# Attention and MLP on one core: normalised rows transposed by DMA instead of TensorE, stores and v loads moved from SyncE to ScalarE

## The chip, the cores and the metric

The kernel runs on one core of a Trainium2 chip. The metric is device time in microseconds (us). The engines of the core are TensorE (PE, matrix products), VectorE (DVE), ScalarE (ACT), GpSimd (POOL) and SyncE (SP, which only issues DMA transfers). ScalarE and GpSimd can issue transfers too. All work from queues of their own, each in program order, and meet through semaphores.

## What is computed

For 8 batches of 8 heads with 576 positions and 64 columns: causal attention with a bias from a running sum, then layer normalisation of the 512 joined columns, then a two-layer MLP with 2048 hidden columns, added back.

```python
cum    = np.cumsum(np.maximum(s, 0.0), axis=-1)
scores = where(causal, -1e9, q @ k.T / 8 + np.minimum(-(cum_i - cum_j), 0.0))
attn   = softmax(scores)
x      = (attn @ v), heads joined            # (8, 576, 512)
xn     = (x - mean(x)) / np.sqrt(var(x) + 1e-6) * g_ln
out    = x + np.maximum(xn @ w_ch1, 0.0) @ w_ch2
```

## The kernel before

The order is written out by hand: every engine runs its instructions in the order in which the program names them. The main loop has 64 slots, one for each batch and head; below, slot h of a batch means the head h = 0 to 7 of the batch whose scores are made in it.

**A slot** first runs `pre(n)`, which names loads, casts and DMA transposes due for later heads. Then come the scores of its head (L312) with their exponentials on ScalarE (L323) and the masking on GpSimd (L331), and, between them, four units of the MLP of the batch before. In the middle stands `pv_next()`: attention times v (L389) for the head two slots back, and its division on VectorE (L397 to L406).

**Layer normalisation.** When the last head of batch b is through `pv_next()`, in slot h = 1 of the next batch, VectorE makes the normalised tiles xn (L451), four of 128 rows and, for odd b, a fifth with the last 64 rows of batches b-1 and b (the mixed tile). The division by the root of the variance is left to the end: it is a factor `rstd`, a power of -0.5 that GpSimd takes (L439) right after the last xn, and that enters when the output tile yo is made (L524). Only batch 1 makes its fourth and fifth tiles a slot later.

**Transposes.** The MLP needs xn with its columns on partitions. `ln_tr` does this for each tile with four 128x128 transposes on TensorE into one PSUM tile `trx` (L484), and a copy from there to xT on VectorE (L100), or on ScalarE (L98) for batches 0 (three of four), 1 and 7. For batches 1 to 6 the tiles 0 and 1 are transposed at the end of slot 2, and 2, 3 and 4 in slot 3; for batch 7 they stand between the last MLP units of batch 6. Batch 0 has its own path (L790 to L793).

**MLP units.** A batch has 32 units in `queue`: 16 of `mlp1` (L497: four products of 512 columns into `ph`, then the ReLU on ScalarE at L507, or on VectorE at L505 for the first unit of a slot), and 16 of `mlp2` (L515: a quarter of the sum for 128 rows into `py`; each fourth unit is followed by yo on VectorE and the store of yo at L542). `ph` and `py` share two PSUM buffers. The units of mlp1 fall in slots 4 to 7, those of mlp2 in slots 0 to 3 of the next batch.

**Loads.** q and k of the later heads are loaded in rows (L164), cast by GpSimd (L176), and transposed by DMA on SyncE into `kq` (L186), four heads at a time over about five slots. The rows of v are loaded by SyncE (L139) in slots 1 to 5 and cast by GpSimd (L102) a slot later. Row loads and v loads share the six buffers of `stage`. So SyncE's queue carries row loads, v loads, DMA transposes and stores, in program order, and an instruction that waits holds up all behind it.

The order inside the slot that the change touches:

```python
lt = {2: (0, 1), 3: (2, 3, 4)}.get(h, ()) if b > 1 else ()
for t in lt:
    ln_tr(b - 1, t, "act" if b == 2 else "dve")
    if t != 1 and t != 4:
        run_units(1)
        nu -= 1
run_units(nu)
```

Of the kernel before, what the change touches and what calls it, by code (L numbers as in the profile page):

```python
# [9 lines left out]
F32 = mybir.dt.float32  # L10
# [5 lines left out]
P = 128  # L16
# [3 lines left out]
def kernel(  # L20
# [11 lines left out]
    nc = tc.nc  # L32
    B, H, S, D = q.shape
# [5 lines left out]
    NF = S // P  # L39
# [13 lines left out]
    QP = S // QT  # L53

    const = ctx.enter_context(tc.tile_pool(name="const", bufs=1))
    stage = ctx.enter_context(tc.tile_pool(name="stage", bufs=6))
    pairs = ctx.enter_context(tc.tile_pool(name="pairs", bufs=4))
    small = ctx.enter_context(tc.tile_pool(name="small", bufs=4))
    xpool = ctx.enter_context(tc.tile_pool(name="xpool", bufs=3))
# [36 lines left out]
    def copy_on(eng, out, in_):  # L96
        if eng == "act":
            nc.scalar.copy(out=out, in_=in_)  # L98
        elif eng == "dve":
            nc.vector.tensor_copy(out=out, in_=in_)  # L100
        else:
            nc.gpsimd.tensor_copy(out=out, in_=in_)  # L102
# [31 lines left out]
    def ld_v(b, t):  # L134
        if b >= B:
            return
        pn = P if t < NF else TL
        tmp = stage.tile([P, H, D], F32, name="vtmp", tag="st")
        nc.sync.dma_start(  # L139
            out=tmp[:pn], in_=v[b, :, t * P : t * P + pn, :].rearrange("h s d -> s h d")  # L140
        )
        loaded["v", b, t] = tmp
# [39 lines left out]
    def tr_rows(gam, t):  # L182
        pn = P if t < NF else TL
        r = ready.pop(("rows", gam, t))
        o = t * 2 * G * P
        nc.sync.dma_start_transpose(  # L186
            out=kq[gam % 2]
            .rearrange("p u h s -> p (u h s)")[:, o : o + 2 * G * pn]
            .rearrange("p (h s) -> p h s", s=pn),
            in_=r[0:pn].rearrange("p u h c -> p (u h c)"),  # L190
        )
# [243 lines left out]
    def ln_rstd(b):  # L435
        n = len(x_tiles(b))
        rs = rstd[:, b, 0:n]
        nc.vector.tensor_scalar_add(out=rs, in0=mvs[b][:, 0:n, 1], scalar1=1e-6)  # L438
        nc.gpsimd.tensor_tensor(out=rs, in0=rs, in1=mhalf[:, 0:n], op=ALU.pow)  # L439

    def ln_aggr(b, t):
# [31 lines left out]
    def ln_first_rstd():  # L473
        for t in range(NF):
            ln_aggr(0, t)
        ln_rstd(0)

    def ln_tr(b, t, eng="dve"):
        if (b, t) not in xns:
            return  # L480
        xn = xns.pop((b, t))
        tr = ps_t.tile([P, KD, P], BF16, name="trx", tag="tr")
        for kd in range(KD):
            nc.tensor.transpose(tr[:, kd, :], xn[:, kd * P : (kd + 1) * P], ident)  # L484
        if t < NF:
            dst = xTs[b][:, :, t * P : (t + 1) * P]
        else:
            dst = xTm[:, :, (b // 2) * P : (b // 2 + 1) * P]
        copy_on(eng, dst, tr)

    first_unit = [False]

# [46 lines left out]
    def batch_units(b):  # L539
        def of_t(t):  # L540
            def put(yo, c0, c1):
                nc.sync.dma_start(out=out[b, t * P : (t + 1) * P, c0:c1], in_=yo)  # L542
            return xb[b][:, t, :], rstd[:, b, t : t + 1], put
        return chunk_units(lambda: xTs[b], of_t)

# [7 lines left out]

    queue = []
    pend = []

    def run_units(n, dve_first=False):
        for i in range(n):
            if queue:
                first_unit[0] = dve_first and i == 0  # L560
                queue.pop(0)()

# [110 lines left out]
    def pre(n):  # L675
# [29 lines left out]
            aug(n // 4 + 1, nc.sync)  # L705
        for gam in range(NPE, NG):
            m = n - 4 * gam
            if m == -6:
                ld_rows(gam, 0), ld_rows(gam, 1)
            elif m == -5:  # L710
                cast_rows(gam, 0), cast_rows(gam, 1)
                ld_rows(gam, 2), ld_rows(gam, 3)
            elif m == -4:
                tr_rows(gam, 0), tr_rows(gam, 1)
                cast_rows(gam, 2), cast_rows(gam, 3)
                ld_rows(gam, 4)
            elif m == -3:
                tr_rows(gam, 2), tr_rows(gam, 3)
                cast_rows(gam, 4)
            elif m == -2:  # L720
                tr_rows(gam, 4)
        for nb in range(2, B):
            m = n - H * nb + (5 if nb == 2 else 7)
            if 0 <= m < NT:
                ld_v(nb, m)
            if 1 <= m <= NT:
                cast_v(nb, m - 1, "pool")

# [16 lines left out]
    for n in range(BH):  # L745
# [64 lines left out]
        if n in PAIRS:  # L810
            qk_pair(PAIRS[n], ("dve", "dve"), ("act", "act"))
        scores(b, h)
        run_units(1, True)
        if h % 2 == 0:
            scores_d(b, h // 2)
# [3 lines left out]
        if n == 9:  # L819
            bias_rows(trc)  # L820
        pend.append((b, h))
        lt = {2: (0, 1), 3: (2, 3, 4)}.get(h, ()) if b > 1 else ()
        for t in lt:
            ln_tr(b - 1, t, "act" if b == 2 else "dve")
            if t != 1 and t != 4:
                run_units(1)
                nu -= 1
        if n == 2 * H + 2:
            for t in range(3, NT):
                ln_xn(1, t)  # L830
        run_units(nu)
        if b > 1 and h == 3:
            run_units(len(queue))
            queue += batch_units(b - 1)
    pv_next()
# [3 lines left out]
    for t in range(NT):  # L839
        ln_xn(B - 1, t + 1)  # L840
        run_units(1)
        ln_tr(B - 1, t, "act")
    run_units(len(queue))
    queue += batch_units(B - 1)
    queue += mixed_units()
# [30 lines left out]
```

The softmax here doesn't subtract the row's maximum and nothing guards it: scores larger than these inputs give would overflow.

## Time and profile before

| what | value |
|---|---|
| time, median of 3 (lowest to highest) | 367.94 us (367.81 to 368.48) |
| span in the profile | 366.8 us |
| VectorE busy | 202.9 us (55%) |
| ScalarE busy | 191.3 us (52%) |
| GpSimd busy | 164.9 us (45%) |
| DMA, mean over the span | 142 GB/s, 52.17 MB |
| DMA, 190 to 220 us | 178 to 208 GB/s |
| TensorE transposes of xn | 144, in 36 tiles of four |
| copies of them to xT and xTm | 23 on VectorE, 13 on ScalarE |
| transfers of SyncE that move: stores of yo / v / rows of q and k / transposes | 37 / 30 / 110 / 55 |

How to read it: a busy share is the time in which the engine had an instruction in hand, over the whole span. The one engine near 100% is TensorE, so what counts is which of its instructions could be missed, and what it would wait for then. In the attention part (up to about 290 us) all engines work; after that come the MLP of batch 7 and that of the mixed rows, in which TensorE has nearly all the work.

### The profile page before, as it was taken

To read this page: it belongs to the slowest core of one execution; us is meant where nothing else is said; L and a number is where in the kernel's file an instruction comes from. 1 tells how busy PE (TensorE), PEld (TensorE's weight loads), DVE (VectorE), ACT (ScalarE), POOL (GpSimd) and SP (SyncE) were. 2 spreads that over 40 slices of the span, in tenths; PEclk is the share of its full clock that TensorE was granted. 3 is DMA by queue.
4 is the path that set the end of the run, shared out by engine and by line. 5 is a ranking of instruction groups with operands and counts; after the bars stand their busy time and mean duration, and the time that the engine had idled before them with its cause. 6 is when DMAs were issued, how large, how long until landed. Compare 5 with 4: busy or idle time off the path is not lost.

```text
span 366.8 us, 8315 instructions
## 1 busy us (share of the span) xinstructions
PE 355.0 (97%) x3017; PEld 197.1 (54%) x3067; DVE 202.9 (55%) x535; ACT 191.3 (52%) x367; POOL 164.9 (45%) x447
## 2 busy tenths in 40 slices
PE   8998999999999999999999999999999999999995
PEld 3677555565555555555455555555555554444444
DVE  7697789684357554944384547743675483112211
ACT  5895988467732673367534753476337522501410
POOL 8854468667633656344675563554852101000000
PEclk9999999999999999999999999999999999999999
DMA  8999999999965999599979986798830011011013
GB/s 144 162 195 178 202 211 193 163 240 176 183 146 141 206 199 181 104 215 163 188 176 213 194 183 140 189 191 182 174 102 2 0 59 57 1 58 59 0 31 86
DMA packets 156653, 52.17 MB, mean 142 GB/s; under 512 B 143641, under 2 KB 151940, under 8 KB 156612
## 3 DMA queue, kind: packets, MB, share of 16 engines
q1 hardware_dynamic: 138868, 43.08, 55.5%
q0 software_dynamic: 17344, 8.03, 18.9%
q8 instruction: 24, 0.39, 0.5%
q10 hardware_dynamic: 400, 0.52, 0.4%
q14 instruction: 17, 0.14, 0.2%
HBM read 37.11 MB, written 9.44 MB: 127 GB/s over the span
## 4 chain that ended last, share of the span: by engine, by line
PE 72%; DVE 7%; DMA 6%; SPq 4%; POOL 4%; issue 3%; ACT 3%; POOLq 0%; ACTq 0%
PE py L515 26%; PE ph L497 25%; PE pot L389 6%; SPq L164 3%; PE sc L312 3%; PE sa L312 3%; PE sb L312 3%; DMA rowtmp<-in_q_dram 2%; PE idle L568 2%; DMA vtmp<-in_v_dram 2%; DVE xn L451 2%; PE trx L484 2%; DVE stats L423 1%; POOL er L331 1%; ACT er L323 1%
## 5 line engine op out<-in xcount | busy, mean ns | idle before, releaser
L515 PE MATMUL py<-w_bf,hT 128*128 128x512 bf16 (+1 forms) x565 | 132.1, 373 | 1.6 <-DVE yo L524 0.4
L497 PE MATMUL ph<-xT,w_bf 128*128 128x512 bf16 x478 | 116.4, 379 | 1.1 <-DVE yo L524 0.2
L507 ACT ACTIVATE hT<-ph 128x512 bf16<-128x512 f32 x102 | 61.0, 598 | 64.4 <-PE ph L497 64.4
L515 PEld LDWEIGHTS <-hT 128*128 128x128 bf16 x592 | 53.5, 98 | 49.1 <-issue 0.9
L497 PEld LDWEIGHTS <-w_bf 128*128 128x128 bf16 x560 | 50.1, 97 | 51.3 <-issue 2.9
L323 ACT ACTIVATE er<-sa 128x512 bf16<-128x512 f32 x64 | 38.2, 597 | 70.9 <-PE sa L312 50.1
L331 POOL TENSOR_SCALAR_AFFINE_SELECT er<-er 128x128 bf16<-128x128 bf16 x216 | 59.7, 300 | 22.5 <-ACT er L323 22.3
L505 DVE TENSOR_SCALAR hT<-ph 128x512 bf16<-128x512 f32 x38 | 26.3, 692 | 56.7 <-PE ph L497 49.0
L176 POOL CAST rows<-rowtmp 128x512 bf16<-128x512 f32 (+1 forms) x55 | 33.5, 609 | 50.7 <-DMA rowtmp<-in_q_dram 46.0
L312 PEld LDWEIGHTS <-kq 68*128 68x128 bf16 x452 | 33.4, 97 | 27.4 <-issue 1.7
L389 PEld LDWEIGHTS <-er 128*128 128x128 bf16 x960 | 37.5, 98 | 14.9 <-issue 0.7
L389 PE MATMUL pot<-v_bf,er 128*128 128x65 bf16 x960 | 40.2, 193 | 0.5 <-PE sd L355 0.3
L397 DVE RECIPROCAL rinv<-pot 128x5 f32<-128x5 f32 x64 | 12.3, 192 | 49.2 <-PE pot L389 48.9
L323 ACT ACTIVATE er<-sc 128x512 bf16<-128x512 f32 x64 | 39.2, 612 | 0.0
L323 ACT ACTIVATE er<-sb 128x512 bf16<-128x512 f32 x64 | 38.4, 599 | 0.3 <-PE sb L312 0.2
L524 DVE SCALAR_TENSOR_TENSOR yo<-py,rstd,xb 128x512 f32<-128x512 f32 x32 | 23.9, 748 | 26.2 <-PE py L515 19.7
L399 DVE TENSOR_TENSOR xb<-pot,rinv 128x256 f32<-128x256 f32 x64 | 27.2, 425 | 2.2
L102 POOL CAST v_bf<-vtmp 128x512 bf16<-128x512 f32 (+1 forms) x30 | 18.5, 617 | 19.6 <-DMA vtmp<-in_v_dram 19.5
L439 POOL TENSOR_TENSOR rstd<-rstd,mhalf 128x4 f32<-128x4 f32 (+1 forms) x8 | 8.8, 1095 | 38.0 <-DVE rstd L438 37.9
L312 PE MATMUL sc<-kq 68*128 68x256 bf16 (+1 forms) x216 | 25.3, 229 | 0.3
L423 DVE BATCH_NORM_STATS2 stats<-xb 128x6 f32<-128x128 f32 (+2 forms) x100 | 25.3, 313 | 0.4
L312 PE MATMUL sb<-kq 68*128 68x64 bf16 (+1 forms) x172 | 24.5, 244 | 0.9 <-DMA kq<-rows 0.6
(101 smaller groups left out, 322.1 us busy)
## 6 DMA issues: line engine op xcount, KB each, us to landing
out_dram<-yo SPq DMA_DIRECT2D x32, 256.0 KB
vtmp<-in_v_dram SPq DMA_DIRECT2D x24, 256.0 KB
rowtmp<-in_k_dram SPq DMA_DIRECT2D x44, 128.0 KB
rowtmp<-in_q_dram SPq DMA_DIRECT2D x44, 128.0 KB
w_bf<-in_moe_w_ch_dram POOLq DMA_DIRECT2D x8, 512.0 KB, 10.7
kp<-in_k_dram POOLq DMA_DIRECT2D x9, 144.0 KB, 6.8
qp<-in_q_dram POOLq DMA_DIRECT2D x9, 144.0 KB, 7.0
v_bf<-in_v_dram POOLq DMA_DIRECT2D x8, 128.0 KB, 8.1
```

What stands on the lines that cost most here:

```text
L176: nc.gpsimd.tensor_copy(out=r[0:pn, :, :, 0:D], in_=loaded.pop(("rows", gam, t))[0:pn])
L312: nc.tensor.matmul(a[:, c + a0 - q0 : c + a1 - q0], lhsT=k_cols(b, h, kb), rhs=cols, start=True, stop=not (pe_mask and diag),)
L323: nc.scalar.activation(out=e[:, o : o + 512], in_=a, func=ACT.Exp, scale=scale)
L331: nc.gpsimd.affine_select(out=e[:, o : o + P], in_=e[:, o : o + P], compare_op=ALU.is_ge, fill=0.0, base=0, pattern=[[1, P]], channel_mult ...
L389: nc.tensor.matmul(pot[:, t, :], lhsT=e[:, o : o + P], rhs=vv[:, kb, h, :], start=(kb == 0), stop=(kb == last),)
L399: nc.vector.tensor_tensor(out=xb[b][:, :, hs], in0=pot[:, 0:NF, 0:D], in1=rinv[:, 0:NF].unsqueeze(2).to_broadcast([P, NF, D]), op=ALU.mult,)
L423: nc.vector.bn_stats(out=st[b][:, t, part, :], in_=x[:, lo:hi])
L497: nc.tensor.matmul(ph, lhsT=w1_bf[:, kd, fb * P : (fb + 1) * P], rhs=xT[:, kd, :], start=(kd == 0), stop=(kd == KD - 1),)
L505: nc.vector.tensor_scalar_max(out=hT[:, fb, :], in0=ph, scalar1=0.0)
L507: nc.scalar.activation(out=hT[:, fb, :], in_=ph, func=ACT.Relu)
L515: nc.tensor.matmul(py[0], lhsT=hT[:, fb, t * P : (t + 1) * P], rhs=w2_bf[:, fb, c0:c1], start=(fb == 0), stop=(fb == FB - 1),)
L524: nc.vector.scalar_tensor_tensor(out=yo, in0=py[0], scalar=rs, in1=x[:, c0:c1], op0=ALU.mult, op1=ALU.add)
```

## The change

The transposes of xn for batches 1 to 7 go from TensorE to DMA transposes on SyncE (`ln_dma`): no product, no PSUM tile, no copy. They are named at the head of slots 2 and 5 (batch 1: slots 2 and 3), for batch 7 where the TensorE transposes stood. To make room on SyncE, the stores of yo for whole batches are issued by ScalarE, each one unit after the unit that made it, and the loads of v are issued by ScalarE after the slot's exponentials, into three buffers of their own, while `stage` keeps four. GpSimd's power moves from right after the last xn (slot 1 or 2) to slot 3 (`ln_pow`), so that GpSimd's queue doesn't wait there for VectorE.

```diff
-    stage = ctx.enter_context(tc.tile_pool(name="stage", bufs=6))
+    stage = ctx.enter_context(tc.tile_pool(name="stage", bufs=4))
...
-        tmp = stage.tile([P, H, D], F32, name="vtmp", tag="st")
-        nc.sync.dma_start(
+        tmp = stage.tile([P, H, D], F32, name="vtmp", tag="v", bufs=3)
+        nc.scalar.dma_start(
...
+    def ln_pow(b):
+        n = len(x_tiles(b))
+        rs = rstd[:, b, 0:n]
         nc.gpsimd.tensor_tensor(out=rs, in0=rs, in1=mhalf[:, 0:n], op=ALU.pow)
...
+    def ln_dma(b, t):
+        if (b, t) not in xns:
+            return
+        if t < NF:
+            dst = xTs[b][:, :, t * P : (t + 1) * P]
+        else:
+            dst = xTm[:, :, (b // 2) * P : (b // 2 + 1) * P]
+        nc.sync.dma_start_transpose(out=dst, in_=xns.pop((b, t)))
...
             def put(yo, c0, c1):
-                nc.sync.dma_start(out=out[b, t * P : (t + 1) * P, c0:c1], in_=yo)
+                stores.append((out[b, t * P : (t + 1) * P, c0:c1], yo))
...
                 first_unit[0] = dve_first and i == 0
+                held = list(stores)
+                stores.clear()
                 queue.pop(0)()
+                for dst, src in held:
+                    nc.scalar.dma_start(out=dst, in_=src)
...
+            if m == -2:
+                tr_rows(gam, 4)
+        if n > 16 and n % H == 2:
+            for t in range(NF if n > 18 else 3):
+                ln_dma(n // H - 1, t)
+        if n == 19:
+            ln_dma(1, 3), ln_dma(1, 4)
+        if n > 19 and n % H == 5:
+            ln_dma(n // H - 1, 4)
...
-            if 0 <= m < NT:
-                ld_v(nb, m)
...
         scores(b, h)
+        for nb in range(2, B):
+            m = n - H * nb + (5 if nb == 2 else 7)
+            if 0 <= m < NT:
+                ld_v(nb, m)
         run_units(1, True)
...
-        lt = {2: (0, 1), 3: (2, 3, 4)}.get(h, ()) if b > 1 else ()
-        for t in lt:
-            ln_tr(b - 1, t, "act" if b == 2 else "dve")
-            if t != 1 and t != 4:
-                run_units(1)
-                nu -= 1
...
         if b > 1 and h == 3:
+            ln_pow(b - 1)
             run_units(len(queue))
...
         run_units(1)
-        ln_tr(B - 1, t, "act")
+        ln_dma(B - 1, t)
+    ln_pow(B - 1)
```

More of the change, by code (lines that the diff above doesn't have):

```diff
@@ L476, in ln_first_rstd @@
         ln_rstd(0)
+        ln_pow(0)
     def ln_tr(b, t, eng="dve"):
@@ L555 @@
     pend = []
+    stores = []
     def run_units(n, dve_first=False):
@@ L707, in pre @@
             m = n - 4 * gam
+            if m == -2:
[7 more added lines that the diff above has]
+            ln_dma(n // H - 1, 4)
+        for gam in range(NPE, NG):
+            m = n - 4 * gam
             if m == -6:
@@ L719, in pre @@
                 cast_rows(gam, 4)
-            elif m == -2:
-                tr_rows(gam, 4)
         for nb in range(2, B):
             m = n - H * nb + (5 if nb == 2 else 7)
-            if 0 <= m < NT:
-                ld_v(nb, m)
             if 1 <= m <= NT:
```

## The prediction

> **What bounds the kernel now.** I read the busy shares first, then TensorE's waits, then the timelines of one batch boundary.
>
> ```profile
> PE 355.0 (97%) x3017; PEld 197.1 (54%) x3067; DVE 202.9 (55%) x535; ACT 191.3 (52%) x367; POOL 164.9 (45%) x447
> ...
> PE   8998999999999999999999999999999999999995
> ```
>
> The first line is the busy time by engine, the second TensorE's share in 40 slices: 9 from the fourth slice to the last but one. A high share of modelled matmuls proves little alone, so I looked at what they wait for. In the list of waits TensorE's own never exceed 1.3 us in total for one cause. Those that bear on the change:
>
> ```profile
> POOL rstd L439 <- DVE rstd L438: 37.9, 7, 13.7
> PEld L312 <- DMA kq<-rows: 1.4, 2, 1.1
> PE sb L312 <- DMA kq<-rows: 0.6, 1, 0.6
> PE py L515 <- DVE yo L524: 0.4, 2, 0.2
> ```
>
> Columns: total us, times, longest. TensorE is the bound and hardly waits; time is to be had only by taking work off it. What the change takes off is seen in the timeline of TensorE for slots 2 and 3 after batch 5:
>
> ```profile
> 226.13 0.62 PE L389 MATMUL pot<-v_bf,er 128*128 128x65 bf16 x15
> 226.58 0.39 PE L484 MATMUL trx<-ident,xn 128*128 128x128 bf16 x4
> 226.81 1.03 PE L515 MATMUL py<-w_bf,hT 128*128 128x512 bf16 x4
> 227.67 0.39 PE L484 MATMUL trx<-ident,xn 128*128 128x128 bf16 x4
> ...
> 229.20 0.39 PE L312 MATMUL sc<-kq 68*128 68x256 bf16 x4
> 229.79 1.89 PE L515 MATMUL py<-w_bf,hT 128*128 128x512 bf16 x8 [0.21 <-DVE yo L524]
> ```
>
> First column start, second duration. From the start of trx to the next product are 226.81 - 226.58 = 0.23 us; other tiles give 0.22. The last line is a wait that the change will make longer.
>
> [...]
>
> **The change part by part.**
>
> *TensorE transposes removed.* Batches 1 to 7 have 4 tiles each and the odd ones a fifth: 28 + 4 = 32 tiles, times 0.222 us = **7.1 us**. All of it lies on the path, as TensorE is. The 22 VectorE copies (416 ns, 9 us) and 10 ScalarE copies (585 ns, 6 us) that go lie beside it: no gain on the path.
>
> *DMA transposes added, batches 2 to 6.* The nearest row is the transposes of kq and the loads that move with them:
>
> ```profile
> L186 SPq DMA_TRANSPOSE kq<-rows x55: 1215/1260/2791, 61.2 to 267.5; - x55
> L139 SPq DMA_DIRECT2D vtmp<-in_v_dram x30: 440/590/1761, 29.4 to 248.4; - x30
> L542 SPq DMA_DIRECT2D out_dram<-yo x32: 332/364/1099, 66.6 to 335.6; - x32
> ```
>
> These are issue times in ns, min, median, max. A kq transpose has 1024 columns, one of xn 512: between 0.63 (by columns) and 1.26 us (fixed per instruction); I take 0.65. Landing follows some 2 us after the issue ends (173.67 + 1.22 to 176.89). After batch 5 the fourth xn is ready at 227.95 (VectorE's timeline), so xT has landed by about 230.6, at the dear end 232.2. MLP1 starts at 235.04, less five transposes at 233.9. Hidden. SyncE per batch: it sheds 5 x 0.59 + 4 x 0.36 = 4.4 us and gains 4.6 x 0.65 to 1.26 = 3.0 to 5.8 us. Nor are its transposes queued behind anything worse than before:
>
> ```profile
> 224.11 0.58 SPq L139 DMA_DIRECT2D vtmp<-in_v_dram  x1
> 229.77 0.36 SPq L542 DMA_DIRECT2D out_dram<-yo  x1
> 230.22 1.33 SPq L186 DMA_TRANSPOSE kq<-rows  x1
> 231.60 0.57 SPq L164 DMA_DIRECT2D rowtmp<-in_k_dram  x1
> ```
>
> Today SyncE stands from 224.7 to 229.8 at a store that waits for yo. With the stores gone it waits for xn until 228, and the row loads behind start near 228.8 instead of 231.6. The shift lets loads run earlier. After batch 3 that same late start (store at 152.01) ended in TensorE waiting for kq between 173 and 177, about 1.5 us by the gaps in its timeline. I count **1.0 us** of it as gained; 0 to 1.5 for the range. Data is 0.13 MB a tile, 0.6 MB a batch onto about 7 MB in 38 us (183 GB/s, while windows reached 209): about 200 GB/s is wanted. Tight, not over.
>
> *Batch 1.* Its fourth xn is made in slot 2 and ends at 78.73; MLP1 starts at 81.24, less five transposes at 80.1. Issue to 79.4, landing at 81.4: TensorE waits **1.2 us** (0.8 to 2.5[...]).
>
> *Batch 7.* Fourth xn 301.45, landed by 304.1; MLP1 at 306.44 less 1.1 = 305.3. Hidden, by 1.2 us at most.
>
> *The yo wait after odd batches.* VectorE runs it behind the xn tiles:
>
> ```profile
> 228.12 0.75 DVE L451 SCALAR_TENSOR_TENSOR xn<-xm,mv,gb 128x512 bf16<-128x512 f32 x1
> 228.79 0.16 DVE L438 TENSOR_SCALAR rstd<-mv 128x5 f32<-128x5 f32 x1
> 228.99 0.75 DVE L524 SCALAR_TENSOR_TENSOR yo<-py,rstd,xb 128x512 f32<-128x512 f32 x1
> ```
>
> The py of slot 3 needs the buffer that this yo frees at 229.74. That chain hangs on the product pot of slot 1, not on the transposes, so TensorE arrives 0.44 us sooner (two transposes) and waits that much more: batches 3 and 5, **0.9 us** given back. With four tiles (even b) yo ends 0.7 us ahead of its need.
>
> *ScalarE's new issues: 30 of v, 32 of yo.* Each costs between nothing (hidden under queued work) and 0.59 or 0.36 us, SyncE's medians[...]. Where ScalarE has slack it doesn't matter. It has little at 40 to 60 us, busy 9.35 and 9.15 of 10 us, and there lie the v loads of slots 11 to 15. Bare, five of 0.59 less its idle 0.54 before the copies that TensorE waits on are 2.4 us. Later the tight place is slot 4: exponentials, a v issue, a store, an exponential, and the ReLU that frees ph, with some 0.5 us to spare against 0.95: bare 0.4 x 6 = 2.4 us. Sum 0 to 4.8; I lean to the hidden end and take **0.8 us**. The store after slot 1 of an odd batch waits for yo until 229.7 and holds the exponentials of slot 3 by a microsecond; their scores' buffers are next wanted in slot 4 (234), their attention in slot 5. Hidden.
>
> *Power two slots late, buffers.* Costs nothing: rstd is wanted by the next slot 0. It frees GpSimd from 37.9 us of waiting (13.7 of it at the end), which moves casts ahead, beside TensorE. Four row buffers suffice: loads 0 and 1 are cast a slot before load 4 wants room; a v buffer is freed two slots before its next load. One unit of delay for a store meets three yo buffers, filled a slot apart. Hidden.
>
> *Sum:* 367.9 - 7.1 - 1.0 + 1.2 + 0.9 + 0.8 = **362.7 us**.
>
> **The rivals.**
>
> *All hidden.* ScalarE's issues cost nothing, the kq wait goes entirely (1.5), and batch 1 waits no more than 0.8: 367.9 - 7.1 - 1.5 + 0.9 + 0.8 = 361.0; without the batch-1 wait 360.2. I call it 360.4.[...] Against it: batch 1's arithmetic.
>
> *ScalarE becomes a second bound.* Issues bare: 367.9 - 7.1 + 0.9 + 1.2 + 4.8 = 367.7 with no gain at kq; with 1.0 there and half of the issues bare, 364.3. I put this case at 366.0. For it: 9.8 us of work in 10 at 40 to 60 us already.
>
> *Slower: issues on ScalarE as slow as SyncE's bad ones.* If each v load holds ScalarE 1.2 us (midway from 0.59 to 1.76): early 5 x 1.2 - 0.54 = 5.5; slots 4 and 5 of five batches 10 x 0.7 = 7.0; with 2.5 for batch 1 and 0.9: 367.9 - 7.1 + 15.9 = 376.7. A starved DMA (200 of 209 GB/s) would look alike. Against it: ScalarE's own ring would hold only v and stores, and 15 of the 30 loads fall in slots 1 to 3, where it is busy 3 to 4 of 10 us.
>
> **How the numbers follow.** The forecast 0.57, all hidden 0.20, second bound 0.13, slower 0.10. The range leaves out the slower case, a tail of the second bound and the edge of all hidden: 359.8 to 367.0. Slower by over 0.2% (368.7): 0.10. Within: 0.04, from the second bound. Faster: 0.86.
>
> **What would show it.** Right: trx only for batch 0 (16 matmuls), TensorE's total down by some 7 us, batch period from 38.1 to about 37.1 us; TensorE waiting for a transfer xT once, near 80 us; py after batches 3 and 5 waiting 0.6 us for yo; no wait of POOL rstd for DVE but the first; SyncE's transposes of 512 columns at 0.65 us. Wrong: transposes of xn at over 1.3 us or landing past 4 us, TensorE waiting for xT in every slot 4, ReLUs waiting behind transfers on ScalarE, or more waits for kq than two.

## The result, and the profile after

| kernel | time, us, median (lowest to highest) | ratio to before, 95% interval |
|---|---|---|
| before, same chip | 367.88 (367.40 to 368.48) | |
| changed | 387.61 (384.88 to 388.52) | 1.0523 (1.0467 to 1.0579) |

Slower by 5.2%, where 362.7 us was forecast. In four of the runs below some executions took over 1.5% more than the fastest of their kernel (of `e6_v_sync_b1_pe` 5 of 20: 372.73 to 378.48 us at a mean clock of 0.984 to 0.995, the others 366.96 to 371.43 us at 0.988 to 1.000): the ratios leave these out, the medians of times don't. The profiled span grew from 366.8 to 386.1 us, by 19.3. The busy shares, TensorE's slices and its granted clock in the page of the changed kernel:

```profile
PE 357.6 (93%) x2892; PEld 193.5 (50%) x2939; DVE 194.4 (50%) x513; ACT 185.3 (48%) x357; POOL 165.5 (43%) x447
...
PE   8899998949999799969999799979999999999996
...
PEclk9999999987999899996999899989999999999999
```

The transposes are gone from TensorE, and yet it is busy 2.6 us longer. Where it was full from the fourth slice on, there are now holes (4, 7, 6, 7, 7), and at most of them, or just behind, the granted clock drops, to 6 to 8 tenths. The holes have names in the list of waits:

```profile
POOL rstd L444 <- DVE rstd L438: 19.1, 2, 13.7
...
PE ph L513 <- ACT hT L523: 9.5, 4, 3.4
...
PE ph L513 <- DMA xT<-xn: 4.8, 1, 4.8
...
PE py L531 <- DVE yo L540: 1.5, 2, 0.7
```

TensorE waits four times for a ReLU (L523, the old L507), 9.5 us in all; before there was no such line. It waits once, in batch 1, for the transposed rows: 4.8 us. Lines have moved: mlp1 is L513, mlp2 L531, yo L540, the transpose L505, the store L583.

What a wait costs beyond itself is seen in TensorE's timeline at the start of MLP1 of batch 3:

```profile
169.49 1.02 PE L513 MATMUL ph<-xT,w_bf 128*128 128x512 bf16 x4
173.87 1.87 PE L513 MATMUL ph<-xT,w_bf 128*128 128x512 bf16 x4 [3.35 <-ACT hT L523]
```

Four products took 1.02 us ahead of the wait and 1.87 behind it: 0.43 us apart instead of 0.216. Behind each of TensorE's five longest waits its clock record stands at 0.50: for 6.83 us behind those of 4.81 and 3.35 us, for 3.41 us behind those of 2.11, 2.10 and 1.94 us. An estimate of this loss from the busy shares: 355.0 - 7.1 for the transposes should give 347.9 us, measured are 357.6, so **some 9.7 us** of the same products at a lower clock. The clock records give much the same: TensorE was busy for 21.2 us of the stretches at 0.50, and with products at half their pace there (0.43 for 0.216 us) half of that, 10.6 us, is lost.

The sum for the span: -7.1 (transposes) -0.6 (the wait for kq that is gone) +9.5 (ReLU) +4.8 (xT) +1.1 (yo, 1.5 against 0.4) +9.7 (clock) = +17.4 of 19.3 us. The rest is in small gaps, the largest a wait of 1.2 us for kq at 13.7 us, ahead of the first moved transfer.

**Why ReLUs come late.** ScalarE's timeline of the same moment (ACTq is its queue issuing a transfer; the number in brackets is idle time):

```profile
162.65 0.36 ACTq L583 DMA_DIRECT2D out_dram<-yo  x1
163.11 0.27 ACT L358 ACTIVATE er<-sd 64x128 bf16<-64x128 f32 x1 [4.58 <-DVE rinv L397]
163.28 0.58 ACT L323 ACTIVATE er<-sa 128x512 bf16<-128x512 f32 x1
163.47 0.37 ACTq L139 DMA_DIRECT2D vtmp<-in_v_dram  x1
163.76 0.59 ACT L323 ACTIVATE er<-sb 128x512 bf16<-128x512 f32 x1
164.24 0.59 ACT L323 ACTIVATE er<-sc 128x512 bf16<-128x512 f32 x1
168.45 0.36 ACTq L583 DMA_DIRECT2D out_dram<-yo  x1
168.92 0.60 ACT L323 ACTIVATE er<-sa 128x512 bf16<-128x512 f32 x1 [4.09 <-DMA rowtmp<-in_q_dram]
...
172.63 0.38 ACTq L583 DMA_DIRECT2D out_dram<-yo  x1
173.06 0.27 ACT L358 ACTIVATE er<-sd 64x128 bf16<-64x128 f32 x1 [2.57 <-DMA rowtmp<-in_k_dram]
173.24 1.06 ACT L523 ACTIVATE hT<-ph 128x512 bf16<-128x512 f32 x2
```

The v load at 163.47 costs nothing: it is issued while the exponential of 163.28 to 163.86 runs, and those around it start 0.48 us apart. All three stores stop everything behind them. The one at 162.65 waited 4.1 us for its yo, which VectorE finished at 162.62. Those at 168.45 and 172.63 had their yo: ScalarE is idle for 4.09 and 2.57 us ahead of what follows, released by *loads of q and k rows on SyncE*, with which a store of yo has nothing to do. The ReLUs at 173.24 stand behind them, and TensorE starts at 173.87.

The instruction records tell what connects the two. Each transfer carries a semaphore, which is updated as it lands (16 times for a row load; the last is its landing here). SyncE's and ScalarE's carry the same eight (numbers 101, 104 to 109 and 118). The 297 transfers of the two engines in the changed kernel fit into one order alone in which the eight take turns, and it is the program's, not that of time: the v load of 163.47 (107) has its turn behind a row load issued at 165.50 (106). Records that wait for a transfer's own semaphore stand right ahead of 222 of SyncE's 230 transfers (all but its first eight) and of 56 of ScalarE's 67, and none of the 289 transfers that reuse a semaphore was issued before its last user had landed (before: none of 257). In the kernel before, where SyncE issued 260 of the 265, that user was eight transfers back, nearly always in its own queue. With two queues sharing the eight, it can be one that the other queue issued just now:

```
transfer on ScalarE   queue free   issued   semaphore   last user, issued        landed
store of yo           164.82       168.45   118         row load of q, 163.78    168.37
store of yo           170.56       172.63   109         row load of k, 167.54    172.55
v load                177.83       178.73   108         row load of q, 174.79    178.64
```

I summed this over each kernel, as **held time**: transfers that started within 0.25 us of that landing while their queue had been free for over 0.3 us, counted from free to landing (some of it may lie behind another wait). Before: none. Changed kernel: 27.4 us of ScalarE in 15 transfers, and 4.9 us of SyncE in 4. Two of the 15, 2.8 us, stood behind an earlier store of ScalarE itself, the others behind a transfer of SyncE. ScalarE has slack for much of it; 9.5 us reach TensorE: each of its four waits for a ReLU ends 1.2 us after such a held store is issued (129.74, 172.63, 214.62 and 256.31 us).

Waits for yo are counted apart: up to 290 us the stores stood another 20.4 us of ScalarE for those, most of it in one store after each of batches 1 to 6, which stood 2.6 to 4.1 us while VectorE made the xn tiles. None of the four ReLU waits follows directly on one.

A starved DMA, the look-alike that the prediction named, doesn't explain it. From 60 to 290 us a row load landed 3.1 us after its issue before and 3.4 us in the changed kernel (medians), and the fastest kernel below moves about as much (55.69 MB, here 56.35) at a higher rate (155 GB/s, here 146).

### The profile page after: what moved, and what is told of

Same layout as the page of the kernel before. It is cut to its first block, busy times and chain, and to the rows that moved or that the text cites. A ratio compares the mean times of both kernels' runs of the same rounds, so it can differ in the third digit from the quotient of the medians.

```text
span 386.1 us, 8154 instructions
## 1 busy us (share of the span) xinstructions
PE 357.6 (93%) x2892; PEld 193.5 (50%) x2939; DVE 194.4 (50%) x513; ACT 185.3 (48%) x357; POOL 165.5 (43%) x447
## 2 busy tenths in 40 slices
DMA packets 174060, 56.35 MB, mean 146 GB/s; under 512 B 161049, under 2 KB 169348, under 8 KB 174020
## 4 chain that ended last, share of the span: by engine, by line
PE 67%; DMA 12%; DVE 9%; ACT 4%; issue 3%; SPq 2%; POOL 1%; ACTq 0%; POOLq 0%
PE ph L513 28%; PE py L531 24%; PE pot L389 5%; DMA rowtmp<-in_k_dram 3%; PE sc L312 3%; PE sb L312 3%; PE sa L312 3%; DMA rowtmp<-in_q_dram 2%; DMA out_dram<-yo 2%; SPq L164 2%; ACT er L323 2%; DMA vtmp<-in_v_dram 2%; DVE xn L456 1%; DVE yo L540 1%; DMA kq<-c 1%
## 5 line engine op out<-in xcount | busy, mean ns | idle before, releaser
L513 PE MATMUL ph<-xT,w_bf 128*128 128x512 bf16 x476 | 125.4, 399 | 16.2 <-ACT hT L523 9.5
L531 PE MATMUL py<-w_bf,hT 128*128 128x512 bf16 (+1 forms) x570 | 131.1, 373 | 2.6 <-DVE yo L540 1.5
L523 ACT ACTIVATE hT<-ph 128x512 bf16<-128x512 f32 x102 | 60.4, 596 | 82.0 <-PE ph L513 79.3
L513 PEld LDWEIGHTS <-w_bf 128*128 128x128 bf16 x560 | 52.0, 101 | 72.1 <-issue 23.0
L331 POOL TENSOR_SCALAR_AFFINE_SELECT er<-er 128x128 bf16<-128x128 bf16 x216 | 61.9, 305 | 52.1 <-ACT er L323 52.0
L531 PEld LDWEIGHTS <-hT 128*128 128x128 bf16 x592 | 53.8, 98 | 53.7 <-issue 2.0
L312 PEld LDWEIGHTS <-kq 68*128 68x128 bf16 x452 | 34.6, 100 | 29.2 <-issue 3.8
L389 PEld LDWEIGHTS <-er 128*128 128x128 bf16 x960 | 37.9, 98 | 14.9 <-issue 2.0
L540 DVE SCALAR_TENSOR_TENSOR yo<-py,rstd,xb 128x512 f32<-128x512 f32 x32 | 23.9, 748 | 27.0 <-PE py L531 22.3
L312 PE MATMUL sa<-kq 68*128 68x512 bf16 x64 | 25.0, 391 | 1.3 <-DMA kq<-c 1.2
```

The source lines that it names most:

```text
L312: nc.tensor.matmul(a[:, c + a0 - q0 : c + a1 - q0], lhsT=k_cols(b, h, kb), rhs=cols, start=True, stop=not (pe_mask and diag),)
L331: nc.gpsimd.affine_select(out=e[:, o : o + P], in_=e[:, o : o + P], compare_op=ALU.is_ge, fill=0.0, base=0, pattern=[[1, P]], channel_mult ...
L389: nc.tensor.matmul(pot[:, t, :], lhsT=e[:, o : o + P], rhs=vv[:, kb, h, :], start=(kb == 0), stop=(kb == last),)
L513: nc.tensor.matmul(ph, lhsT=w1_bf[:, kd, fb * P : (fb + 1) * P], rhs=xT[:, kd, :], start=(kd == 0), stop=(kd == KD - 1),)
L523: nc.scalar.activation(out=hT[:, fb, :], in_=ph, func=ACT.Relu)
L531: nc.tensor.matmul(py[0], lhsT=hT[:, fb, t * P : (t + 1) * P], rhs=w2_bf[:, fb, c0:c1], start=(fb == 0), stop=(fb == FB - 1),)
```

## The experiments

My theory L was this sharing. The rivals changed with the question: S, everything is SyncE's lateness; I, ScalarE's 62 issues are the load; V, the v loads cost ScalarE their time by themselves. Ratios are to the kernel before on the same chip; "held" is ScalarE's held time.

### Which part costs

Four kernels each undo a part of the change. First the DMA transposes with stores and v loads back on SyncE (`e1_tr_dma_only`) and the stores alone back (`e3_stores_sync`):

```diff
-stores.append((out[b, t * P : (t + 1) * P, c0:c1], yo))
+nc.sync.dma_start(out=out[b, t * P : (t + 1) * P, c0:c1], in_=yo)
 # e1 only: the v loads as in the kernel before, six buffers
```

> The changed kernel with the stores of yo and the loads of v back on SyncE (six shared buffers), the DMA transposes and the late power kept. Theory L (every hardware transfer of SyncE and ScalarE takes the next of eight shared completion semaphores and first waits until the transfer eight places earlier in program order has landed, so ScalarE stands waiting for SyncE's late row loads, and its ReLUs come late): ScalarE issues no transfer now, so no ReLU waits behind one; SyncE carries about 34 us of issues in 37 and TensorE waits for xT after batches 1, 3 and 5 instead; 370 to 380 us. Rival S (SyncE is late because four transposes of 1.22 us and their waits for xn stand in its queue; ScalarE has no part in it): as slow as the changed kernel or slower, 385 to 395. Rival I (ScalarE's 62 issues of 0.37 us are the load): 361 to 364.

> The changed kernel with only the stores back on SyncE. Theory L: the waits in front of the ReLUs of slot 4, where a store stood, go; those at v loads stay; SyncE is held by stores that wait for yo, so xT and row loads come later: 374 to 386 us, less ReLU waiting than the 9.5 us of the changed kernel. Rival S: slower than the changed kernel, 388 to 395. Rival I: half of the issues gone, half of the loss, about 375.

Measured: 400.35 us, 1.0899 (1.0809 to 1.0989), and 402.04 us, 1.0948 (1.086 to 1.1037). Both are worse than the full change, by more than any of the three theories said. Waits of TensorE in the first:

```profile
PE ph L513 <- DMA xT<-xn: 22.1, 7, 5.3
```

Seven waits, one per batch: a store on SyncE that waits for yo now stands ahead of the transposes, and yo is made behind the xn tiles. So stores issued by SyncE at once don't go with the DMA transposes. No late ReLU was left here, nor in the second kernel, which has 25.0 us in seven such waits. There the 30 v loads stayed on ScalarE and were held for 1.7 us in all, so v loads on ScalarE don't by themselves bring the late ReLUs. (TensorE came later to the ReLUs by its waits for xT, though, which leaves ScalarE time.)

Then the moves to ScalarE with the transposes on TensorE (`e2_scalar_moves_only`), and the v loads alone back on SyncE (`e4_v_sync`):

```diff
 # e2
-ln_dma(n // H - 1, t)      # and the other calls
+ln_tr(b - 1, t, "act" if b == 2 else "dve")   # as before
 # e4
-nc.scalar.dma_start(out=tmp[:pn], in_=v[b, ...])
+nc.sync.dma_start(out=tmp[:pn], in_=v[b, ...])   # named in pre(n) again
```

> The changed kernel with the transposes back on TensorE, stores and v loads on ScalarE as changed. Theory L: ScalarE still waits for transfers of SyncE to land, but SyncE is less late without its 5 us of transposes a batch: waits of 1 to 2 us at slot 4, 369 to 377 us. Rival S: SyncE is relieved of 62 issues and nothing is added, 366 to 368. Rival I: 372 or more, with no wait of ScalarE that ends with a landing.

> The changed kernel with only the v loads back on SyncE. Theory L: the store in slot 4 still waits for a landing, now with SyncE later by five more issues a batch: 382 to 392 us, ReLU waits as before or longer. Rival S: slower than the changed kernel, 388 to 395. Rival I: half of the issues gone, about 375.

Measured: 384.89 us, 1.0428 (1.0343 to 1.0513), and 374.42 us, 1.0166 (1.0092 to 1.0239). In the first, with no DMA transpose of xn at all, most of the loss is there:

```profile
PE trx L490 <- ACT er L358: 12.7, 6, 2.8
```

The transposes on TensorE need the PSUM buffer that ScalarE's exponential of sd frees, and that exponential stands behind a transfer. But this is not the sharing in the main: in five of the six waits, 10.3 us, the store waited for its yo (the one issued at 158.27 got its yo at 158.24, while its semaphore was free at 153.81); only in the first, 2.4 us, a v load waited for a row load. Held is 9.9 us. So ScalarE's moves cost by themselves, but here mostly by another wait than in the changed kernel, and the time of this kernel is no evidence for L. L's 369 to 377 us failed with it, and so did S's 366 to 368.

In the second, held falls from 27.4 to 7.8 us, the ReLU wait from 9.5 to 0.5 us, and 13 us of time come back. By L I had expected the v loads to matter little (382 to 392); with the stores on ScalarE too they were the largest single item. Rival I's number (about 375) was met, but by that rival the two kernels above should have been fast as well (361 to 364 and about 375 us).

### What holds ScalarE

`e5_v_early` names the v loads ahead of the slot's SyncE transfers, `e7_stores_4_late` issues the stores four units late:

```diff
 # e5, in pre(n), ahead of the first transfer
+ld_v(nb, m)
 # e7, in run_units
-held = list(stores); stores.clear(); queue.pop(0)()
-for dst, src in held: nc.scalar.dma_start(out=dst, in_=src)
+count[0] += 1; queue.pop(0)()
+while stores and stores[0][2] <= count[0] - 4: ...   # then issued on ScalarE
```

> The changed kernel with one thing moved: each v load stays on ScalarE but is written ahead of the slot's SyncE transfers in the program. Theory L (hardware transfers of SyncE and ScalarE use eight completion semaphores in turn, in the order of the program, so a v load waits on ScalarE until the eighth transfer before it has landed): the transfer that a v load waits for is now one of the slot before, landed long ago, so ReLUs come in time: TensorE's wait for ScalarE's ReLU falls from 9.5 us to under 4 us and the time to 374 to 381 us (374.4 with the v loads on SyncE, which also leaves SyncE some issues more). Rival V (the v issue itself, 0.37 us beside the exponentials, is what delays the ReLUs): as the changed kernel, 385 to 389 us. The wait for xT in batch 1 (4.8 us) stays in both.

> The changed kernel with the stores issued four units late instead of one, so that ScalarE never meets a store whose yo VectorE has yet to make behind the xn tiles. If the wait of ScalarE's store for yo starts the delay (exponentials late, then GpSimd's casts, then SyncE's transposes and loads, then ScalarE's waits for their landings): the wait of ScalarE for out<-yo (3.8 us in the page) goes and the time falls to 376 to 383 us. If the delay comes from the landings alone: within 2 us of the changed kernel, 386 to 389 us, ReLU wait near 9.5 us.

Measured: 386.37 us, 1.0513 (1.0479 to 1.0547), and 386.4 us, 1.0487 (1.0433 to 1.0541). Neither differs from the changed kernel. In the first the v loads are held 3.3 instead of 7.2 us, but the stores still 18.4: the wait stayed with the stores. The number of L for it failed, and that of V (385 to 389) was met. In the second held is 24.3 us and the ReLU wait 12.9. Nor did it free ScalarE of yo: five stores still stand 2.5 to 4.0 us while their semaphore has long been free (one from 158.19 to 162.16, last user landed at 156.21), since four units are about the slot that VectorE spends on xn. So the share of that wait in the loss isn't told by this kernel.

`e10_gp_moves` issues both from GpSimd, whose 36 transfers in the changed kernel carry eight other semaphores (110 to 117); `e11_v_gp` only the v loads:

```diff
-nc.scalar.dma_start(out=tmp[:pn], in_=v[b, ...])
+nc.gpsimd.dma_start(out=tmp[:pn], in_=v[b, ...])
 # e10 also: the stores, four units late, on nc.gpsimd
```

> The changed kernel with v loads and stores issued from GpSimd instead of ScalarE (the stores four units late, so that GpSimd doesn't wait for yo). GpSimd's transfers complete on eight semaphores of their own, and ScalarE issues none. Theory L (ScalarE's transfers wait for landings of SyncE's, since both draw on the same eight semaphores): no ReLU comes late for a transfer, TensorE's wait for ReLUs falls from 9.5 us to under 1 us, batch 1's wait for xT (5 to 6 us) stays, time 370 to 377 us. Rival D (the DMA engines are starved and every landing late, whoever issues): the ReLU wait goes, but waits for xT and kq take its place, time over 382 us.

> The changed kernel with only the v loads issued from GpSimd; the stores stay on ScalarE, one unit late. With the v loads on SyncE it took 374.4 us. Theory L: again fewer of ScalarE's transfers meet a young predecessor on their semaphore (two or three a slot 4 become one), and SyncE has five issues a batch less: 371 to 376 us. Rival V (v loads land late because they start late, wherever they are issued from): 383 to 389 us.

Measured: 400.01 us, 1.0868 (1.0811 to 1.0925), and 404.99 us, 1.101 (1.097 to 1.105). Both times are far from those of L. The rival of the first, D (the DMA engines are starved and every landing is late), had over 382 us with waits for xT in the place of those for ReLUs, and both came. The waits of the second, with the stores alone left on ScalarE:

```profile
PE ph L513 <- ACT hT L523: 13.4, 4, 4.3
PE ph L513 <- DMA xT<-xn: 8.5, 2, 7.9
```

Held is 24.2 us, all by stores, each by a landing of SyncE's. With both off ScalarE, held is nothing and TensorE's list of waits has no ReLU at all. That part of L holds. What the time shows is another bottleneck: a v load issued from GpSimd takes 914 ns of that engine (median), 30 of them 26.4 us, and its masks, with the products pot behind them, and its row casts come late. SyncE's transposes of kq wait for those casts (40.2 us of SyncE's queue in the first kernel, 12.9 in the changed one), and the transposes of xn stand behind them. Row loads landed 3.7 us after their issue in the first, against 3.4 in the changed kernel: a part of D may be in it. These two times say nothing on ScalarE.

### Batch 1, and what a transpose costs SyncE

The page of instructions by line, for L505 of the changed kernel (ns, least, median, most):

```profile
L505 SPq DMA_TRANSPOSE xT<-xn x28: 1188/1217/2442, 74.9 to 322.6; - x28
```

A transpose of 512 columns takes SyncE 1.22 us to issue, like one of kq with 1024 (1.26): at these two widths a fixed cost per instruction, where I had taken 0.65. In batch 1 this adds up (SyncE's timeline, changed kernel):

```profile
74.92 3.81 SPq L505 DMA_TRANSPOSE xT<-xn  x3
78.79 0.58 SPq L164 DMA_DIRECT2D rowtmp<-in_k_dram  x1
...
81.19 2.44 SPq L505 DMA_TRANSPOSE xT<-xn  x1
```

The fourth tile was ready at 79.43, its transpose was issued only from 81.19 to 83.63, behind four row loads that stood behind three transposes, and TensorE waited until 85.67. `e6_v_sync_b1_pe` (v loads on SyncE, batch 1 on TensorE) and `e8_v_sync_b1_pe_late` (the same with the stores four units late):

```diff
 # v loads as in the kernel with them on SyncE, and
-for t in range(NF if n > 18 else 3): ln_dma(n // H - 1, t)
-if n == 19: ln_dma(1, 3), ln_dma(1, 4)
+for t in range(NF if n > 18 else 0): ln_dma(n // H - 1, t)
+lt = {2: (0, 1), 3: (2, 3, 4)}.get(h, ()) if b == 2 else ()   # ln_tr(b - 1, t, "act")
```

> The changed kernel with the v loads issued from SyncE again (374.4 us by itself) and, besides, batch 1's five tiles transposed on TensorE and copied by ScalarE, as in the kernel before. Theory B (batch 1's transposes by DMA come 5 to 6 us late[...]): the wait for xT near 80 us goes (5.9 us), with it the slow products after it (20 products or so at 0.43 instead of 0.22 us, 4 us), against 5 x 0.22 = 1.1 us of transposes: 365 to 368 us. Rival: SyncE's lateness only moves on (xT waits in later batches, seven of 5 us when the stores are on SyncE): over 371 us.

> Three things together: v loads from SyncE, batch 1's transposes on TensorE, stores four units late on ScalarE. If each of the waits is separate, this keeps 27 transposes off TensorE (27 x 0.222 = 6.0 us) with the waits for yo (two of about 0.7 us) left: 361 to 364 us, faster than the kernel before (367.9). If late stores bring nothing once the v loads are on SyncE: the same as the kernel with the first two alone, 365 to 368 us.

Measured: 369.28 us, 1.0015 (0.999 to 1.0041), and 369.63 us, 1.004 (1.0019 to 1.006). Batch 1 gives back 1.5%, and the change is level with the kernel before. Late stores bring nothing; the first kernel came out a little above its range (365 to 368), the second above both of its ranges. ScalarE was held for 8.4 and 13.5 us here, and TensorE waited only 1.2 and 0.2 us for ReLUs: held time is no measure of the loss, what counts is what stands behind it.

`e12_pairs` puts two tiles of xn into one transpose of 1024 columns, xT laid out by tiles; `e9_late_sync` asks the opposite, whether SyncE could carry it all with single transposes once its stores come four units late:

```diff
 # e12, on e6
-xTs[b] = xtp.tile([P, KD, 512], BF16, ...)
+xTs[b] = xtp.tile([P, NF, KD, P], BF16, ...)
-nc.sync.dma_start_transpose(out=dst, in_=xns.pop((b, t)))
+if t % 2 == 1:
+    nc.sync.dma_start_transpose(
+        out=xTs[b][:, t - 1 : t + 1].rearrange("p t k c -> p (t k) c"),
+        in_=xn2[b, t // 2].rearrange("p t c -> p (t c)"))
 # e9, on e1: stores four units late, on nc.sync
```

> The kernel with v loads on SyncE and batch 1's transposes on TensorE (1.0015 of the kernel before), with two tiles of xn in one DMA transpose of 1024 columns (xT laid out by tiles), so two instead of four instructions per batch. If the issue time is a fixed cost per instruction: L505 shows 1.2 to 1.3 us each, about 17 instructions instead of 23, xT lands 2.4 us sooner, the last wait for xT (1.4 us) and the late ReLUs (1.2 us) shrink: 363 to 367 us. If it goes by data: 2.4 us each, the time as before, 367 to 370 us.

> The DMA transposes alone (stores and v loads issued from SyncE, six row buffers, late power; 400.4 us when the stores follow one unit late or at once), with the stores issued four units late on SyncE, so that SyncE meets no store whose yo is still to come behind the xn tiles. Theory Y (with everything on SyncE the loss is the store that waits for yo at the head of the queue, ahead of the transposes of xn and the row loads): seven waits for xT (22.1 us) shrink to two or three of under 3 us, time 368 to 376. Rival N (SyncE's own issue time is too much: 1.22 us for each of 34 transposes more): the waits for xT stay at 4 to 5 us in each batch, time 392 to 402.

Measured: **362.83 us, 0.9894 (0.9857 to 0.9932)**, and 381.78 us, 1.0376 (1.0335 to 1.0417). In the first:

```profile
L510 SPq DMA_TRANSPOSE xT<-xn x12: 1231/1258/1532, 112.7 to 299.3; - x12
```

Twice the columns at 1.26 us instead of 1.22: of these two widths, the cost is per instruction. TensorE no longer waits for xT or for a ReLU, and held is 1.4 us. The second lies between its theories: the late stores bring 18.6 of the 400.35 us back, but two waits for xT (5.5 us) and six for kq (7.0 us) remain, so SyncE alone can't carry it in time.

`e15_pairs_b1_dma` is the paired kernel with batch 1 by DMA too (its diff is the reverse of the one for batch 1 above):

> The kernel with paired transposes with batch 1's tiles by DMA too (tiles 0 and 1 together in slot 2, 2 and 3 together in slot 3). With single transposes the step from TensorE to DMA in batch 1 cost 5.5 us (1.0166 against 1.0015). Its last transpose still hangs on the fourth xn of slot 2 and starts behind the same row loads, so the wait for xT stays, shorter by up to 1.2 us: 366 to 368.5 us. If the lateness of batch 1 was SyncE's three transposes of 3.8 us ahead: one pair ahead takes 1.3, all later ones start 2.5 us sooner, and the wait is 2 to 3 us: 363.5 to 366 us.

Measured: 370.21 us, 1.0091 (1.0063 to 1.012): 7.4 us for this one batch, above both ranges.

```profile
PE ph L525 <- DMA xT<-xn: 5.7, 1, 5.7
```

Fewer transposes ahead did not help: the wait is as long as with single ones. Batch 1's fourth tile comes a slot later than those of other batches, and its transpose is issued from 80.08 to 82.20, behind four row loads and a v load, while TensorE stands ready at 80.49.

### The v loads on ScalarE, once more

`e13_pairs_v_act` puts the v loads of the paired kernel back on ScalarE, as the change has them. `e17_v_act_slot_top` then names them, and the stores, at the head of the slot, ahead of SyncE's transfers:

```diff
 # e17, on e13, ahead of pre(n)
+for dst, src in stores: nc.scalar.dma_start(out=dst, in_=src)
+stores.clear()
+ld_v(nb, m)   # for the slot's v tile
```

> The kernel with paired transposes (two tiles of xn in one DMA transpose, batch 1 on TensorE, v loads on SyncE: 0.9894 of the kernel before, 362.8 us) with the v loads back on ScalarE as in the changed kernel. Theory L (ScalarE's loss is waiting for landings of late SyncE transfers on a shared semaphore): SyncE is 2.4 us a batch earlier than in the changed kernel and sheds 30 v issues, its transfers land in time, and the 13 us that the v loads cost in the changed kernel shrink to under 4 us: 361 to 367 us. Rival V (the v loads on ScalarE cost 13 us by their own issues and starts): 372 to 378 us.

> The kernel with paired transposes and v loads on ScalarE (1.0535 of the kernel before, 386.6 us), with the slot's v load and the stores of the slot before written at the head of the slot, ahead of SyncE's transfers of that slot. Same transfers, same engines, same issues; what changes is that the eighth transfer before each of them on the shared semaphores now lies a whole slot (some 4.6 us) back instead of inside the burst of row loads just issued. Theory L (ScalarE loses its time waiting for those landings, which take 4 to 6 us in the burst): ScalarE's waits for landings fall from 19.5 us to under 6, TensorE's for ReLUs from 14 us to under 3, time 361 to 370 us. Rival V (30 v loads cost ScalarE their time wherever they stand): 380 to 388 us.

Measured: 386.55 us, 1.0535 (1.0513 to 1.0556), and 393.92 us, 1.0689 (1.0631 to 1.0747). All four numbers failed. The first shows that fewer issues on SyncE don't help: held is back at 19.5 us and the ReLU wait at 14.0 us in 8 waits, and seven of the eight end 1.2 to 1.3 us after a held transfer of ScalarE is issued. Row loads issued eight in a burst still land late (one issued at 165.89 landed at 170.73, 4.8 us). The second did not take the wait away, so it decides nothing: held is 21.5 us, and the stores at the head of the slot wait for yo ahead of all exponentials.

**Left open.** That ScalarE is held by landings of SyncE's transfers, and that ReLUs and TensorE wait behind it, is shown by the traces; that it goes with the transfers, by the kernels with v on SyncE or with all on GpSimd. No kernel kept both the 30 v loads and the stores on ScalarE without the sharing: two tried and didn't take the wait away. What part of the 13 us (24 in the paired kernel) would remain without it isn't measured. The waits for yo alone aren't the loss: the paired kernel with v on SyncE has as many (19.9 us up to 290 us, against 20.4 in the changed kernel) and is faster than the kernel before. Whether they add to the loss where the sharing is at work stays open.

### What is left

`e16_pairs_yo_first` makes the fifth xn tile of batches 3 and 5 behind the next yo, `e14_pairs_early_pow` puts the power back where it was, `e18_best` does both, all on the paired kernel:

```diff
 # e16
-for t in range({1: 3, B - 1: 1}.get(pb, NT)): ln_xn(pb, t)
+for t in range({1: 3, B - 1: 1}.get(pb, NF)): ln_xn(pb, t)
 run_units(nu)
+if b > 2 and h == 1: ln_xn(b - 1, NF)
 # e14: the power again in ln_rstd, no ln_pow
```

> The kernel with paired transposes with the fifth xn tile of batches 3 and 5 made behind the next yo on VectorE instead of ahead of it. The wait of py for yo (2.3 us, two times) should fall to under 0.4 us and the time by 1.5 to 2.5 us: 360.3 to 361.3 us. If TensorE then waits elsewhere (scores' buffers, ReLUs): within 0.7 us of 362.8.

> The kernel with paired transposes with GpSimd's power back right behind the rstd of the last xn tile, as in the kernel before. If the late power brings nothing to the end (as predicted): 362 to 364.5 us, POOL's wait of rstd rises from 21 to some 38 us. If GpSimd's casts behind the power matter: the row casts come up to 3 us later in slot 2, SyncE's kq transposes with them, and TensorE waits for kq again: 365 to 369 us.

> The two improvements of the paired kernel together: the fifth xn tile behind yo (361.2 us, ratio 0.9837) and the power right behind rstd again (361.9 us, ratio 0.9864, TensorE waiting for yo 1.3 us instead of 2.3). If both were real and separate: 359.8 to 361 us. If the early power only moved the yo wait by chance and the fifth tile's move takes all of it: 361 to 362 us.

Measured: 361.19 us, 0.9837 (0.9805 to 0.9869); 361.89 us, 0.9864 (0.9846 to 0.9882); 360.01 us, **0.9783 (0.9747 to 0.982)**. The wait that the first takes away, in the paired kernel:

```profile
PE py L543 <- DVE yo L552: 2.3, 2, 1.1
```

It is gone in the first kernel. The intervals of the first two overlap that of the paired kernel (0.9857 to 0.9932), so neither step alone is told apart from it with certainty; both together are. The early power is at least no worse than the late one. The last kernel's page:

```profile
PE 348.6 (97%) x2930; PEld 191.1 (53%) x2959; DVE 194.4 (54%) x513; ACT 188.1 (53%) x362; POOL 165.5 (46%) x447
...
PE   8998999999999999999999999999999999999995
```

TensorE is full again, at a clock of 1.000, and busy 6.4 us less than before (355.0 to 348.6, with 3017 and 2930 matmul records beside 3067 and 2959 of weight loads). This kernel beats both of the original ones.

## Why the prediction was wrong

**TensorE transposes removed, 7.1 us: right.** Only batch 0's 16 matmuls of trx remain. With batch 1 left on TensorE, 27 tiles x 0.222 = 6.0 us go, and the best kernel shows 6.4 of busy time.

**ScalarE's new issues, 0 to 4.8 us, taken at 0.8: the step that failed.** The price of the issue was right, and so was its hiding, an estimate that the trace before did not show: 0.375 and 0.363 us at the median, 0.73 and 1.39 at most, between exponentials that don't notice (the rival with issues of 1.2 us was wrong in its mechanism, if right in its sign). What was missing is the wait ahead of the issue. I asked only whether yo would be there, and against a slower case I argued that "ScalarE's own ring would hold only v and stores". So it did (queue q10 of the page moved 16.00 MB, which is what those transfers carry), but SyncE's and ScalarE's transfers took turns on the same eight semaphores. The eighth transfer before it, on another engine, was on no view that I had read; in the trace before, where SyncE issues nearly everything, no transfer was held by it. It measured 27.4 us of ScalarE and 9.5 us of TensorE; the v loads' part cost 13 us in time. The hold for yo was mis-sized as well: it was to delay the exponentials of slot 3 by a microsecond, and after batch 3 it stood ScalarE's queue for 4.1 us, with slot 2's exponential of sd behind it. With the transposes on TensorE it wasn't hidden: TensorE waited 10.3 us behind such stores. That a ReLU waits behind a transfer was named as a sign of being wrong.

**DMA transposes, issue 0.65: mis-sized.** 1.22 us, close to the dear end of my range (1.26). For batches 2 to 7 it stayed hidden as said: no wait for xT there in the changed kernel. But SyncE's balance turned: 4.6 x 1.22 = 5.6 us gained per batch against 4.4 shed. Pairing brought the ratio from 1.0015 to 0.9894.

**Batch 1, 1.2 us (0.8 to 2.5): mis-sized.** The wait was 4.8 us. The working let the fourth transpose start when its xn was ready; it took no account of three transposes of 1.22 us and four row loads ahead of it in SyncE's own queue. With the slower products behind it the batch cost 1.5%.

**What a stall does to the clock: not priced.** Each term was counted as its own length. Some 9.7 us of slower products came on top, behind waits as short as 1.94 us.

**kq wait, 1.0 gained: right in kind.** No wait of sb for kq<-rows remains among TensorE's waits, where it was 0.6 us, and 1.4 for the weight loads.

**The yo wait, 0.9 given back: right.** 1.1 us more than before over the two batches named; 1.9 us more (2.3 in all) in the paired kernel, where TensorE comes earlier.

**Power and buffers at nothing: right.** GpSimd's wait fell from 37.9 to 19.1 us, less than said, since the 13.7 at the end stayed, and the time didn't gain by it.

With the v loads on SyncE, batch 1 on TensorE and paired transposes, the kernel takes 362.83 us. That it meets the forecast of 362.7 is partly chance: it forgoes five tiles and has the yo waits longer.

## What to carry to other kernels

Before moving a transfer to another engine's queue, look up what its issue waits for besides its data: here two queues drew on the same eight semaphores, and in 15 transfers, for 27.4 us, ScalarE stood until the transfer eight back in program order, 13 times one of the other queue, had landed. A cheap, hidden issue (0.37 us here) is no argument if a wait can stand ahead of it on an engine whose results TensorE needs (9.5 us of TensorE's waits). Count a DMA transpose as it was measured here, by instruction (1.22 us with 512 columns, 1.26 with 1024) and not by columns, and count a stall of TensorE with the slower products behind it (some 9.7 us). And look in each kernel for what a held transfer waited for: the changed kernel's ReLUs stood behind the shared semaphores, the TensorE transposes of the kernel with the moves alone mostly behind data not yet made.

## What the runs showed of the hardware

- A DMA transpose issued by SyncE took 1.22 us with 512 columns (changed kernel) and 1.26 us with 1024 (kernel before, and paired kernel), at the median.
- A transfer of v took 0.375 us to issue from ScalarE (changed kernel), 0.61 us from SyncE (with the v loads there and batch 1 on TensorE) and 0.914 us from GpSimd (v loads and stores there), at the median.
- From issue to landing a row load between 60 and 290 us took 3.1 us at the median in the kernel before and 3.4 us in the changed one; the two behind whose landing the stores of 168.45 and 172.63 were issued took 4.6 and 5.0 us (163.78 to 168.37, 167.54 to 172.55).
- After waits of 3.35 and 4.81 us (changed kernel) TensorE's products of 512 columns came 0.43 us apart instead of 0.216, and its clock record stood at half for 6.83 us; after waits of 1.94, 2.10 and 2.11 us it stood at half for 3.41 us. Not each wait of that length went with it. With the moves alone one of 2.79 us, between 230 and 240 us, was followed by half the clock (means of 0.96 and 0.87 from 230 to 240 and 240 to 250 us), one of 2.83 us, between 150 and 160 us, was not (1.00 from 150 to 170 us).
- SyncE's and ScalarE's transfers took turns on the same eight semaphores (297 of 297 in the changed kernel), GpSimd's 36 on eight others; in the changed kernel 15 transfers of ScalarE whose queue had been free for 0.3 to 4.1 us were issued 0.07 to 0.10 us after the landing of their semaphore's last user.
